# Order of the four array tiles in the seven-product steps, and moved query and key turns, in a thresholded-attention and bilinear-FFN kernel

## The chip, the cores and the metric

The kernel runs on one core of a Trainium2 chip. The metric is the device time of one execution in microseconds (us). The core has a matrix engine (PE, with its weight loads shown apart as PEld), a vector engine (DVE), an activation engine (ACT), a general engine (POOL) and a sync engine (SP) that here issues nearly all DMA transfers. Each engine works through its own instructions in program order, and waits for semaphores that others raise.

## The reference

Everything is 32-bit float. There are 8 batches, 8 heads, 576 positions and 64 columns a head.

```python
scores = scale * np.matmul(q, k.transpose(0, 1, 3, 2))
thresh = np.max(scores, axis=-1, keepdims=True) - tau
scores = np.where(scores >= thresh, scores, -1000000000.0)
attn = np.exp(scores - np.max(scores, axis=-1, keepdims=True))
attn = attn / (np.sum(attn, axis=-1, keepdims=True) + 1e-09)
x = np.matmul(attn, v)          # then (B,H,S,D) -> (4608, 512)
out = (x @ w_a) * (x @ w_b) @ w_out   # 512 -> 1536 -> 512
```

## The kernel before

**Units and slots.** Two heads of one batch make a pair, 32 pairs in all. A pair has 576 query rows: four blocks of 128, and a tail of 64 that it shares with its neighbour pair in one more block (block number `NT`). This gives 144 units (pair, block). The main loop runs over slots `g`; slot `g` computes the scores of unit `g` and works on older units: `turn_blocks` of unit `g-1`, `turn_back` of `g-2`, and the product with v (`weighted`) with a lag of three slots. The first eight units (`g < BY_PE`) turn their weights on PE (`turn_pe`), all later ones through DVE and a DMA to DRAM and back.

**A slot's attention work.** `scores` (matmuls at L404) writes two PSUM tiles. DVE takes the row maxima (L411), ACT the exponentials (L432), DVE applies the threshold mask and sums (L435, in `weigh`), DVE inverts the sums (L448), ACT scales (L454), DVE transposes in 32x32 blocks (L502), SP moves the result to DRAM (`swap`) and back (`wT`). `product` (L546) multiplies with v, and `settle` copies the result out of PSUM (ACT L553, DVE L554).

**Keys and queries.** For the first four pairs, `prep_pe` turns q and k on PE (L378) and `prep_copy` copies them from PSUM on DVE (L383). For all later pairs `prep` is one DVE transpose in place (L365) of a tile that SP loaded some slots earlier; q is turned one slot before its first use (the second half of an odd pair two slots before), k two slots before. In program order the q turn stands behind `turn_blocks` and ahead of the masks of the same slot, and the k turn stands behind the masks and ahead of the FFN work of that slot's second portion.

**FFN.** The FFN is a generator that `advance` moves on by a number of columns in several portions of each slot. A block is 256 rows of x. Plain products are at L828, with copy and multiply at L834 and L836. From the second group of batches on, two thirds of the first layer use the seven products of a 2x2 scheme (`sevens_of`, matmuls at L724, sums at L756 to L798, with L789, L794 and L798 on DVE). The second layer does so too (L894, sums at L857). At the end, when attention is done, only FFN remains.

**The array in four tiles.** Nearly all matmuls have 64 rows and 64 output columns, so they use one quarter of the 128x128 array: row half `r` (which partitions are read) and column half `c` (which output partitions are written). One step of `product` in `sevens_of` issues four matmuls, in the order (r,c) = 00, 01, 10, 11, with 128 columns each. Each 32-bit matmul of the program appears in the trace as two records.

**What sets the order.** The program order is fixed: `keep_order` ties each instruction to the one before it on its engine. PSUM has four tiles of two banks, handed out by `banks` in program order; a matmul into a reused tile waits for the engines that read it last. SP's transfers are queued by `post` and let out by `pump` as PE's columns pass.

**Tails of the first four pairs.** `parts(i, NT)` lists two products with v, one for each pair of a pair of pairs, with 32 moving columns in each matmul (`width` is 64 for the two row halves together).

Of the kernel before, what the change touches and what calls it, by code (L numbers as in the profile page):

```python
# [34 lines left out]
RAWS = 4  # L35
# [19 lines left out]
def kernel(  # L55
# [38 lines left out]
    nc = tc.nc  # L94
# [69 lines left out]
    def flush(*keys):  # L164

        while any(key in keys for key, _, _ in bulk):
            pump(1, False)
# [86 lines left out]
    def load_weights(limit, engine=nc.sync, most=NPIECES):  # L254

        behind = None
        if most < NPIECES:
            behind = next(x.name for x in reversed(nc.cur_bb.bb.instructions) if x.engine == mybir.EngineType.PE)
        while most and (len(raws) - len(taken) < limit or extra) and state["loaded"] < state["due"]:
            most -= 1  # L260
            n = state["loaded"]
            if len(raws) - len(taken) < limit:
                raw = work.tile([P, CW, 2], U32, tag="xT", bufs=XT_BUFS, name="raw")
            else:
                raw = taken[n] = extra.pop(0)
            src = pieces[n][1]
            for r, part in enumerate(src):
                dst = raw.rearrange("p f w -> p (f w)")[r * D:r * D + P // len(src)]
                if len(src) == 2:
                    dst = dst.rearrange("p (k f) -> p k f", k=2)  # L270
                moved = engine.dma_start(dst, part)
                if behind and r == 0:
                    tc.add_manual_dep(
                        moved.ins, behind,
                        mybir.DependencyInfo(mybir.DependencyClass.Sync, mybir.DependencyReason.DATA),
                        reason="pace")
            raws[n] = raw
            state["loaded"] = n + 1
# [103 lines left out]
    def prep_copy(mT, tp):  # L382
        nc.vector.tensor_copy(mT.rearrange("p (c k) -> p c k", c=2), tp)  # L383
# [56 lines left out]
    def reciprocal(i, u, engine):  # L440
        ws, sums = weights[i, u]
        n = len(ws)
        if engine is nc.scalar:
            nc.scalar.activation(sums[:, 0:n], sums[:, 0:n], AF.Copy, bias=1e-9)
        else:
            nc.vector.tensor_scalar_add(sums[:, 0:n], sums[:, 0:n], 1e-9)
        rcp = small.tile([P, 2], FP32, tag="rcp", name="rcp")
        nc.vector.reciprocal(rcp[:, 0:n], sums[:, 0:n])  # L448
        weights[i, u] = (ws, rcp)
# [38 lines left out]
    def parts(i, u):  # L488

        if i < HP:  # L490
            return {1: [(i, 0)], 3: [(i, 1)], NT: [(i, 2), (i + 1, 2)]}.get(u, [])
        return {1: [(i, 0)], NT if i % 2 == 0 else 3: [(i, 1)]}.get(u, [])

    def width(i, h):
        return (HALF, HALF, TAIL)[h] if i < HP else (HALF, HALF + TAIL)[h]

    def turn_blocks(i, u):

        ws, _ = weights.pop((i, u))
        t = whole.pop((i, u))  # L500
        for w in ws:
            nc.vector.transpose(w, w)  # L502
        swap = scratch.tile([G, P, NSLOT * Q], FP32, tag="swap" if u < NT else "swapt", name="swap")
        swaps[i, u] = swap
        for g in range(G):
            if u < NT:
                moves = [(swap[g].rearrange("(r p) e -> p r e", p=Q),
                          t[g * Q:(g + 1) * Q].rearrange("p (r s) e -> p r (s e)", r=G))]
            else:
                moves = []  # L510
                for m in range(2):
                    j = g // 2 ^ m
                    moves.append((swap[2 * m + g % 2, j * D:(j + 1) * D].rearrange("(r p) e -> p r e", p=Q),
                                  t[g * Q:(g + 1) * Q, m * NB:(m + 1) * NB].rearrange("p (r s) e -> p r (s e)", r=2)))
            post(("tw", i, u), *moves)
# [78 lines left out]
    def weighted_unit(i, u):  # L594
# [10 lines left out]
        if hp == HP - 1:  # L605
            state["rows"] = u + 1
            if u == 0:
                blocks.append(((x_of[b, 0], state["xs"]), ("first", b, 0)))

    def weighted(i, h):  # L610

        b, hp = pairs[i]
        flush(("v", i), ("wT", i if i >= HP or h < 2 else i - i % 2, h))
        n = width(i, h)
        if h < 2:
            groups = G + (n > HALF)
            wT = [turned.pop((i, 2 * h + y))[:, 0:groups] for y in range(2)]
        else:
            t = turned[i - i % 2, NT]
            wT = [t[:, i % 2 * 2 + y:i % 2 * 2 + y + 1] for y in range(2)]  # L620
            if i % 2:
                del turned[i - 1, NT]
        pv = product([lambda rows, s, t=t: t[rows, :, s] for t in wT], loaded[i]["v"], n)
        read = [], []
        settled_of[i] = settled_of.get(i, 0) + n
        if settled_of[i] == S:
            del loaded[i], prepared[i]
        if h < 2:
            if hp == 0:
                x_of[b, h] = x_tile("xT")  # L630
            settle(x_of[b, h][:, hp, :], pv, 0, P, read)
            settled[b, h] = hp + 1
            if hp == HP - 1:
                del settled[b, h]
                complete.append((x_of.pop((b, h)), ("half", b, h)))
        if n % HALF:
            t = b % GT
            if hp == 0 and t == 0:
                xtail_of[b // GT] = x_tile("xt")
            settle(xtail_of[b // GT][:, hp, t * TAIL:(t + 1) * TAIL], pv, (n - TAIL) // 2, n // 2, read)  # L640
            if hp == HP - 1 and t == GT - 1:
                complete.append((xtail_of.pop(b // GT), ("tail", b - t, 0)))
# [40 lines left out]
    def sevens_of(x, hg, plain):  # L683
# [29 lines left out]
        def product(m, out, fresh, last, groups=two):  # L713
            w, moving = products[m]
            nf = 2 * len(groups)
            left = whole = nf * HP * P
            for f in range(nf):
                g, y = groups[f // 2], f % 2
                for k in range(HP):
                    for r in range(2):  # L720
                        rows = slice(r * D, (r + 1) * D)
                        for c in range(2):
                            w0 = y * P + c * D
                            nc.tensor.matmul(out[c * D:(c + 1) * D, r, f * P:(f + 1) * P],  # L724
                                             w[g][k][rows, w0:w0 + D], moving[k][rows],
                                             start=(fresh and k == 0 and f == 0),
                                             stop=(k == HP - 1 and f == nf - 1),
                                             skip_group_check=True)
                    left -= P
                    if left:  # L730
                        yield P, left, whole
# [359 lines left out]
    for g in range(len(units) + PV_LAG):  # L1091
# [37 lines left out]
            advance(PORTIONS[0] * pace)  # L1129
        if g > BY_PE and g <= len(units):  # L1130
            turn_blocks(*units[g - 1])
        for p in range(HP, NPR):
            for name, d in (("q0", 1), ("q1", 1)):
                if g == (second if name == "q1" else first)[p] - d - (name == "q1" and p % 2):
                    prep(p, name)
        load_weights(RAWS if g < 9 else 3, most=1)
        if here:
            weigh(i, u)
        if here and g < BY_PE:
            reciprocal(i, u, nc.vector)  # L1140
        if 0 < g <= BY_PE:
            turn_pe(*units[g - 1])
        if g < 3:
            prep_copy(*prep_pe(g + 1, "k"))
        for p in range(HP, NPR):
            for name, d in (("k", 2),):
                if g == (second if False else first)[p] - d:
                    prep(p, name)
        if g > BY_PE:
            n = g - PV_LAG  # L1150
            held = 0.0
            now = parts(*units[n]) if BY_PE <= n < len(units) else []
            if now:
                held = 384 - (PORTIONS[2] + PORTIONS[3]) * pace + NSLOT * sum(width(*x) for x in now) // 2
                held = min(max(held, 0.0), 384)
            advance(PORTIONS[1] * pace - held)
            for p, h in now:
                if pairs[p][1] == 0:
                    make_x(2 if h == 1 and p >= HP and pairs[p][0] % GT == 0 else 1)
                make_room()  # L1160
                weighted(p, h)
                passed(NSLOT * width(p, h) // 2)
                running["owed"] -= NSLOT * width(p, h) // 2
            if back and back[0] > 0 and units[g - 2] != (0, NT):
                turn_back(*units[g - 2])
# [89 lines left out]
```

## Time and profile before

| what | value |
|---|---|
| median of 3 runs | 1408.98 us (1406.78 to 1411.38) |
| device time of the profiled execution | 1411.51 us |
| its span in the trace | 1409.7 us |
| PE busy, instructions | 1363.7 us (97%), 33980 matmul records |
| DVE busy | 1019.9 us (72%) |
| ACT busy | 678.2 us (48%) |
| POOL busy | 492.8 us (35%) |
| granted TensorE clock, mean | 0.999 |

Busy time is the union of an engine's instructions. Matmuls are pipelined and four run side by side, so the mean length of one (269 ns for 128 columns) is not what it costs; the distance between starts is. "Idle before" and "waits" name the engine or transfer whose semaphore came last. Times in the trace are counted from the start of the span.

### The profile page before, as it was taken

The page shows a single profiled execution, that of the slowest core. Times are in us where ns is not written, and L with a number is a line of the kernel's source. Part 1 is how long each engine was busy: PE and PEld are TensorE (multiplying, and loading weights), DVE is VectorE, ACT ScalarE, POOL GpSimd, SP SyncE. Part 2 cuts the span into 40 slices and gives each one's busy share as a digit, 9 for nine tenths or more (in the row PEclk, how much of TensorE's full clock was granted, in tenths as well). Part 3 has the DMA queues.
Part 4 walks back from the last instruction along what each step waited for, and adds up shares of the span by engine and source line. Part 5 has one row for each costly group of instructions (what it writes and reads, how often), then busy time and mean ns, then how long its engine had stood idle before and what let it go on. Part 6 is the DMA issues. An engine that isn't in the chain of part 4 may idle for free.

```text
span 1409.7 us, 76575 instructions
## 1 busy us (share of the span) xinstructions
PE 1363.7 (97%) x33980; PEld 1242.7 (88%) x33980; DVE 1019.9 (72%) x2212; ACT 678.2 (48%) x1245; POOL 492.8 (35%) x675
## 2 busy tenths in 40 slices
PE   6789999999999999999999999999999999999998
PEld 5678577899889899899997899998899899799998
DVE  6999877787777878776767776777777776745424
ACT  5887555545554555544444545454545455431110
POOL 2774442424150606060515142331515060708100
PEclk9999999999999999999999999999999999999999
DMA  9977776667666775675555765567655775550000
GB/s 206 241 209 221 202 211 160 177 167 191 175 155 162 195 196 150 172 199 152 142 149 145 191 168 154 137 165 184 181 137 148 201 191 152 136 153 18 4 19 18
DMA packets 327450, 223.23 MB, mean 158 GB/s; under 512 B 171600, under 2 KB 311632, under 8 KB 327120
## 3 DMA queue, kind: packets, MB, share of 16 engines
q1 hardware_dynamic: 323936, 216.95, 59.4%
q8 instruction: 268, 4.39, 1.3%
q10 hardware_dynamic: 3184, 1.38, 0.4%
q14 instruction: 62, 0.51, 0.1%
HBM read 128.58 MB, written 89.65 MB: 155 GB/s over the span
## 4 chain that ended last, share of the span: by engine, by line
PE 88%; DVE 5%; DMA 3%; SPq 2%; issue 1%; ACT 1%; DVEq 0%; ACTq 0%
PE pab L724 29%; PE po L894 21%; PE pab L828 18%; PE sc L404 10%; PE pv L546 9%; SPq L144 1%; DVE tw L435 1%; DVE mx L411 1%; DMA raw<-in_moe_w_b_dram 1%; DMA raw<-in_moe_w_a_dram 1%; DMA wT<-swap 1%; DVE low L311 1%; DVE tw L502 1%; DMA kT<-in_k_dram 0%; PE tp L483 0%
## 5 line engine op out<-in xcount | busy, mean ns | idle before, releaser
L454 ACT ACTIVATE tw<-tw,rcp 128x576 f32<-128x576 f32 x272 | 196.0, 768 | 211.8 <-DVE rcp L448 211.8
L411 DVE TENSOR_REDUCE mx<-sc 128x1 f32<-128x576 f32 x288 | 204.6, 751 | 119.3 <-PE sc L404 118.7
L432 ACT ACTIVATE tw<-sc,bias,scalars 128x576 f32<-128x576 f32 x288 | 239.4, 831 | 10.6 <-DMA qT<-in_q_dram 0.7
L686 POOL TENSOR_TENSOR h<-h,u 128x512 f32<-128x512 f32 x28 | 35.1, 1277 | 597.5 <-DVE h L798 416.0
L435 DVE SCALAR_TENSOR_TENSOR tw<-sc,thr,tw 128x576 f32<-128x576 f32 x288 | 220.3, 796 | 9.9 <-ACT tw L432 9.8
L894 PE MATMUL po<-wo_sb,h 64*64 64x256 f32 (+1 forms) x3408 | 212.9, 367 | 0.0
L502 DVE STREAM_TRANSPOSE tw<-tw 128x576 f32<-128x576 f32 x272 | 194.4, 752 | 0.8 <-ACT tw L454 0.8
L894 PEld LDWEIGHTS po<-wo_sb,h 64*64 64x64 f32 x3408 | 169.7, 133 | 16.6
L404 PE MATMUL sc<-kT,qT 64*64 64x288 f32 x2016 | 176.1, 404 | 4.3 <-DVE xt L554 1.4
L546 PE MATMUL pv<-wT,vm 64*64 64x128 f32 (+3 forms) x5040 | 167.4, 273 | 4.0 <-issue 3.4
L546 PEld LDWEIGHTS pv<-wT,vm 64*64 64x64 f32 x5040 | 156.5, 133 | 13.3 <-issue 7.9
L894 PE MATMUL po<-sums_u,h 64*64 64x256 f32 x2448 | 157.8, 376 | 0.8 <-DVE h L836 0.8
L857 POOL TENSOR_TENSOR h<-h 128x256 f32<-128x256 f32 x168 | 117.2, 731 | 111.7 <-PE po L894 100.4
L724 PE MATMUL pab<-xU,wb_sb 64*64 64x128 f32 x4352 | 139.4, 269 | 0.7 <-issue 0.7
L894 PEld LDWEIGHTS po<-sums_u,h 64*64 64x64 f32 x2448 | 125.4, 133 | 14.2 <-DVE h L836 1.3
L724 PEld LDWEIGHTS pab<-xU,wb_sb 64*64 64x64 f32 x4352 | 133.9, 133 | 3.3 <-issue 1.2
L404 PEld LDWEIGHTS sc<-kT,qT 64*64 64x64 f32 x2016 | 107.1, 133 | 26.2 <-issue 6.8
L431 ACT ACTIVATE bias<-mx,scalars 128x1 f32<-128x1 f32 x288 | 82.7, 287 | 63.3 <-DVE mx L411 62.8
L553 ACT COPY xT<-pv 128x128 f32<-128x128 f32 (+1 forms) x68 | 17.6, 258 | 198.2 <-PE pv L546 198.2
L724 PE MATMUL pab<-xS,wa_sb 64*64 64x128 f32 x2176 | 107.7, 269 | 0.0
L554 DVE COPY xT<-pv 64x128 f32<-64x128 f32 (+1 forms) x136 | 38.1, 280 | 82.2 <-PE pv L546 80.6
L535 ACT COPY kept<-po 128x512 f32<-128x512 f32 x65 | 34.8, 535 | 120.9 <-PE po L894 107.0
(159 smaller groups left out, 2470.4 us busy)
## 6 DMA issues: line engine op xcount, KB each, us to landing
wT<-swap SPq DMA_DIRECT2D x242, 288.0 KB, 3.8
swap<-tw SPq DMA_DIRECT2D x480, 144.0 KB, 3.1
vm<-in_v_dram SPq DMA_DIRECT2D x128, 72.0 KB, 2.2
swap<-tw SPq DMA_DIRECT2D x128, 72.0 KB, 3.0
kT<-in_k_dram SPq DMA_DIRECT2D x112, 72.0 KB, 3.3
wT<-swap SPq DMA_DIRECT2D x56, 144.0 KB, 3.4
out_dram<-kept SPq DMA_DIRECT2D x27, 256.0 KB, 3.6
qT<-in_q_dram SPq DMA_DIRECT2D x112, 40.0 KB, 2.5
```

Source lines behind the costliest of these rows:

```text
L404: nc.tensor.matmul(sc[m][o * D:o * D + wide, c], qT[r, q0:q0 + wide], kT[r, c * SH:(c + 1) * SH], start=True, stop=True)
L411: nc.vector.tensor_reduce(mx[:, c], sc[j], axis=AX.XY, op=ALU.max)
L431: nc.scalar.activation(bias[:, j:j + 1], mx[:, j:j + 1], AF.Copy, scale=e_nscale)
L432: nc.scalar.activation(wb[j], sb[j], AF.Exp, bias=bias[:, j:j + 1], scale=e_scale)
L435: nc.vector.scalar_tensor_tensor(out=wv, in0=sb[j], scalar=thr[:, j:j + 1], in1=wv, op0=ALU.is_ge, op1=ALU.mult, accum_out=sums[:, j:j + 1])
L454: nc.scalar.activation(w, w, AF.Copy, scale=rcp[:, j:j + 1])
L502: nc.vector.transpose(w, w)
L546: nc.tensor.matmul(pv[c * D:(c + 1) * D, y], vm[rows, s], wT[y](rows, s), start=(s == 0), stop=(s == NSLOT - 1))
L724: nc.tensor.matmul(out[c * D:(c + 1) * D, r, f * P:(f + 1) * P], w[g][k][rows, w0:w0 + D], moving[k][rows], start=(fresh and k == 0 and f ...
L828: nc.tensor.matmul(pab[c:c + columns(), r], w[rows, f // n, k, fs + c:fs + c + columns()], moving, start=(k == 0), stop=(k == H - 1))
L857: (nc.vector if state["over"] else nc.gpsimd).tensor_tensor(*a, **kw)
L894: nc.tensor.matmul(po[c * D:(c + 1) * D, r, y, cut], ht[rows, t0:t0 + D], other[rows, f, cut], start=(f == 0), stop=(f == NF // 2 - 1))
```

## The change

Four edits, in the order of the diff.

1. The tails of the first four pairs: two products of 36 matmuls with 32 moving columns become one of 36 matmuls with 64 (`weighted_tails`), in two places. The copies out of PSUM change from two on ACT (128x32) and four on DVE (64x32) to two and two of 64x64.
2. In a step of the seven products the four tiles come in the order 00, 11, 01, 10. The number of matmuls and their operands stay.
3. `prep` of q comes behind the weight load and the masks of its slot; `prep` of k comes behind the FFN work of the slot's second portion (and ahead of the product with v).
4. In slots 0 to 2, the PE turn of the next key stands ahead of `turn_pe`, and its copy out of PSUM is on ACT, where it was behind `turn_pe` and on DVE.

On PE, ACT, POOL and SP the instruction streams are otherwise in the same order as before; on DVE only the turns and copies named change place.

```diff
-            return {1: [(i, 0)], 3: [(i, 1)], NT: [(i, 2), (i + 1, 2)]}.get(u, [])
+            return {1: [(i, 0)], 3: [(i, 1)], NT: [(i, 2)]}.get(u, [])
...
-        return (HALF, HALF, TAIL)[h] if i < HP else (HALF, HALF + TAIL)[h]
+        return (HALF, HALF, 2 * TAIL)[h] if i < HP else (HALF, HALF + TAIL)[h]
...
+    def tails(x, pv, hp, c0, c1):
+        copies = [(nc.scalar.copy if j == c else nc.vector.tensor_copy)(
+            x[j * D:(j + 1) * D, hp + c, c0:c1], pv[c * D:(c + 1) * D, j]) for c in range(2) for j in range(2)]
...
+    def weighted_tails(i):
+        b, hp = pairs[i]
+        flush(("v", i), ("v", i + 1), ("wT", i, 2))
+        t = turned.pop((i, NT))
+        pv = banks(TAIL, "pv")
+        for s in range(NSLOT):
+            for j in range(2):
+                rows = slice(j * D, (j + 1) * D)
+                for c in range(2):
+                    nc.tensor.matmul(pv[c * D:(c + 1) * D, j], loaded[i + c]["v"][rows, s],
+                                     t[rows, 2 * c:2 * c + 2, s], start=(s == 0), stop=(s == NSLOT - 1))
...
                 for k in range(HP):
-                    for r in range(2):
+                    for r, c in ((0, 0), (1, 1), (0, 1), (1, 0)):
                         rows = slice(r * D, (r + 1) * D)
-                        for c in range(2):
-                            w0 = y * P + c * D
-                            nc.tensor.matmul(out[c * D:(c + 1) * D, r, f * P:(f + 1) * P],
...
+                        w0 = y * P + c * D
+                        nc.tensor.matmul(out[c * D:(c + 1) * D, r, f * P:(f + 1) * P],
...
+        load_weights(RAWS if g < 9 else 3, most=1)
+        if here:
+            weigh(i, u)
         for p in range(HP, NPR):
             for name, d in (("q0", 1), ("q1", 1)):
                 if g == (second if name == "q1" else first)[p] - d - (name == "q1" and p % 2):
                     prep(p, name)
-        load_weights(RAWS if g < 9 else 3, most=1)
-        if here:
-            weigh(i, u)
         if here and g < BY_PE:
             reciprocal(i, u, nc.vector)
+        if g < 3:
+            kT, tp = prep_pe(g + 1, "k")
+            nc.scalar.copy(kT.rearrange("p (c k) -> p c k", c=2), tp)
         if 0 < g <= BY_PE:
             turn_pe(*units[g - 1])
-        if g < 3:
-            prep_copy(*prep_pe(g + 1, "k"))
-        for p in range(HP, NPR):
-            for name, d in (("k", 2),):
-                if g == (second if False else first)[p] - d:
-                    prep(p, name)
...
             advance(PORTIONS[1] * pace - held)
+            for p in range(HP, NPR):
+                for name, d in (("k", 2),):
+                    if g == (second if False else first)[p] - d:
+                        prep(p, name)
             for p, h in now:
```

More of the change, by code (lines that the diff above doesn't have):

```diff
@@ L608, in weighted_unit @@
                 blocks.append(((x_of[b, 0], state["xs"]), ("first", b, 0)))
+    def tails(x, pv, hp, c0, c1):
+        copies = [(nc.scalar.copy if j == c else nc.vector.tensor_copy)(
+            x[j * D:(j + 1) * D, hp + c, c0:c1], pv[c * D:(c + 1) * D, j]) for c in range(2) for j in range(2)]
+        for n, a in enumerate(copies):
+            for m, b in enumerate(copies[:n]):
+                if (n in (0, 3)) != (m in (0, 3)):
+                    tc.declare_no_dep(a.ins, b.ins, reason="partitions of their own")
+    def weighted_tails(i):
[9 more added lines that the diff above has]
+                                     t[rows, 2 * c:2 * c + 2, s], start=(s == 0), stop=(s == NSLOT - 1))
+        if hp == 0 and b % GT == 0:
+            xtail_of[b // GT] = x_tile("xt")
+        t = b % GT
+        tails(xtail_of[b // GT], pv, hp, t * TAIL, (t + 1) * TAIL)
+        for p in (i, i + 1):
+            settled_of[p] = settled_of.get(p, 0) + TAIL
+            if settled_of[p] == S:
+                del loaded[p], prepared[p]
     def weighted(i, h):
+        if i < HP and h == 2:
+            return weighted_tails(i)
         b, hp = pairs[i]
-        flush(("v", i), ("wT", i if i >= HP or h < 2 else i - i % 2, h))
+        flush(("v", i), ("wT", i, h))
         n = width(i, h)
[L615 to L622, printed above, removed]
+        groups = G + (n > HALF)
+        wT = [turned.pop((i, 2 * h + y))[:, 0:groups] for y in range(2)]
         pv = product([lambda rows, s, t=t: t[rows, :, s] for t in wT], loaded[i]["v"], n)
@@ L719, in product @@
                 for k in range(HP):
-                    for r in range(2):
+                    for r, c in ((0, 0), (1, 1), (0, 1), (1, 0)):
                         rows = slice(r * D, (r + 1) * D)
-                        for c in range(2):
-                            w0 = y * P + c * D
[L724 to L728, printed above, removed]
+                        w0 = y * P + c * D
+                        nc.tensor.matmul(out[c * D:(c + 1) * D, r, f * P:(f + 1) * P],
+                                         w[g][k][rows, w0:w0 + D], moving[k][rows],
+                                         start=(fresh and k == 0 and f == 0),
+                                         stop=(k == HP - 1 and f == nf - 1),
+                                         skip_group_check=True)
                     left -= P
```

## The prediction

> **What bounds the kernel now.** I read the page first (engines, slices, chain), then the groups of PE by shape, PE's timeline in two places, the waits of DVE, and the timeline of single slots.
>
> ```profile
> span 1409.7 us, 76575 instructions
> ...
> PE 1363.7 (97%) x33980; PEld 1242.7 (88%) x33980; DVE 1019.9 (72%) x2212; ACT 678.2 (48%) x1245; POOL 492.8 (35%) x675
> ...
> DMA  9977776667666775675555765567655775550000
> ...
> PE 88%; DVE 5%; DMA 3%; SPq 2%; issue 1%; ACT 1%; DVEq 0%; ACTq 0%
> ```
>
> PE is the bound, and DMA is full in the first two slices (to 70 us). What a matmul costs is the distance between starts, read from the timeline of PE in the last stage (L724) and around three units' scores (L404):
>
> ```profile
> 1293.96 0.27 PE L724 MATMUL pab<-xT,wa_sb 64*64 64x128 f32 x1
> 1293.96 0.31 PE L724 MATMUL pab<-xS,wa_sb 64*64 64x128 f32 x3
> 1294.07 0.27 PE L724 MATMUL pab<-xT,wa_sb 64*64 64x128 f32 x1
> 1294.07 0.31 PE L724 MATMUL pab<-xS,wa_sb 64*64 64x128 f32 x3
> ...
> 225.85 1.15 PE L404 MATMUL sc<-kT,qT 64*64 64x288 f32 x16
> 233.30 1.15 PE L404 MATMUL sc<-kT,qT 64*64 64x288 f32 x16
> ```
>
> Four records, one on each tile of the array, start together, and the next four come 0.109 us later. Such a quartet takes 0.058 us at 64 columns, 0.109 at 128, 0.136 at 160, 0.216 at 256 and 0.2425 at 288 (starts in the trace). Counting all 33980 records at these rates gives 1322 us. The other 88 us of the span are stalls: 57 before 200 us, 31 after, and those 31 lie in some forty places of 0.1 to 1.6 us, not in the rate.
>
> Three kinds of stall concern the change. A late transfer holds DVE at a turn, and the FFN's copies behind it hold a PSUM tile that the next scores need:
>
> ```profile
> DVE qT L365 <- DMA qT<-in_q_dram: 7.0, 7, 1.8
> ...
> DVE kT L365 <- DMA kT<-in_k_dram: 4.9, 3, 2.1
> ```
> ```profile
> 959.54 0.78 DVE L365 STREAM_TRANSPOSE kT<-kT 128x576 f32<-128x576 f32 x1 [2.11 <-DMA kT<-in_k_dram]
> ...
> 960.24 1.18 DVE L789 TENSOR_TENSOR h<-h,pab 128x1024 f32<-128x1024 f32 x1
> ...
> 961.48 0.95 PE L404 MATMUL sc<-kT,qT 64*64 64x288 f32 x11 [1.15 <-DVE h L789]
> ```
>
> In the first slots scores wait for the key's copy, and the second tail product waits for a PSUM tile:
>
> ```profile
> 15.07 0.73 DVE L383 COPY kT<-tp 128x576 f32<-128x576 f32 x1
> ...
> 15.87 2.30 PE L404 MATMUL sc<-kT,first_u 64*128 64x288 f32 x8 [3.09 <-DVE kT L383]
> ```
> ```profile
> 121.12 1.25 PE L546 MATMUL pv<-sums_u,vm 64*64 64x32 f32 x72
> ...
> 123.50 1.35 PE L546 MATMUL pv<-sums_u,vm 64*64 64x32 f32 x72 [1.13 <-ACT h L834]
> ...
> 160.38 2.30 PE L546 MATMUL pv<-wT,vm 64*64 64x32 f32 x144
> ```
>
> **Part 1, the tile order: 0 us.** It touches all of L724: 15232 records in 3808 quartets, 3808 x 0.109 = 415 us. Each tile keeps its own work, so in a steady stretch only the phase between tiles can move. That the new order runs at full rate is shown once: a unit made of two pairs' tails issues its scores in exactly the order 00, 11, 01, 10. The unit at 233.30 is such a one, the one at 225.85 has 00, 10, 01, 11, and both take 1.15 us for 16 records. So zero is taken from the nearest row, though that row has 288 columns and L724 has 128, where weight loads come more than twice as often. Bounds: below, the part of a quartet that does not grow with columns (0.2158 - 2 x 0.1067 = 2.4 ns, from 256 against 128 columns), 3808 x 2.4 ns = 9 us of gain; above, one more start step (7 ns between neighbours in a quartet) each time, 3808 x 7 ns = 27 us of loss.
>
> [...]
>
> **Part 2, the turns of q and k: -2.2 us.** No instruction is added. 56 turns of q (0.40 to 0.51 us) go behind two masks (L435, 0.8 us each), 28 turns of k (0.77 us) behind the FFN's DVE work. SP's transfers keep their order, so no transfer starts elsewhere. Gains, by the stalls of PE in the trace: at 449.1, 933.5 and 1091.9 a q transfer held the masks for 1.2 to 1.8 us and the scores then waited for the masked tile (0.46, 0.33 and 0.73 us); at 818.2, 961.5 and 1119.2 a k transfer held L789 or L794 for 0.8 to 2.1 us (0.50, 1.35 and 1.0 us). Together 4.4 us; I take 3.4, since behind the FFN work the k turn still stands ahead of the copies of the product with v (L554), which the same scores wait for. Loss: the next scores need the q that now ends when the second mask ended before. In 50 of 56 slots that mask ended 0.3 us or more before the next scores, so nothing is late. In six it ended after they began (by 0.09 to 0.68 us). In three of those the masks now fill the time in which q is awaited; the others (154.0, 333, 482) cost 0.7, 0.2 and 0.3 us, 1.2 in all. Elsewhere the cover is the 0.3 to 3.5 us between mask and scores; if it went, 56 x 0.45 = 25 us would be at stake. What waits behind k on DVE is L554, then the inversions (L446, L448), for which ACT's L454 waits; its block is turned only in the next slot, where DVE waited for L454 once (0.8 us in all). Net -2.2, range -4.4 to +1.2.
>
> **Part 3, keys in slots 0 to 2: -0.8 us.** ACT's copy (0.64 us, as the first key's at L1069) follows the second exponential (ends 13.69), so scores start near 14.4 instead of 15.87: -1.5. In slot 2 the scores no longer wait for the copy at 24.2 but for the masks of slot 1 (22.94 less 1.5): about -3. Slot 3 likewise: -3.9. But these slots also convert weights that arrive at a fixed pace, one half piece each 1.1 us from 25 to 70 us, DMA full. In slot 4 ACT reads its third piece at 48.10, and that piece landed at 47.38. So ACT can be 0.7 us earlier there, and no more; its exponentials follow. I take 0.8; with all cover wrong it is 3.9, with transfers later still 0. ACT's three copies (1.9 us) stand ahead of the conversions that wait for the same pieces.
>
> **Part 4, tails: -1.9 us.** 288 records become 144. The first place loses a block of 1.35 us; its wait for L834 passes to the FFN's next matmul (L828), which takes that PSUM tile. Counted 1.3. The second falls from 2.30 to about 1.2 us (64 columns: 72 records in 1.28, at 39.73), but a DMA wait follows at 172.5 (1.1 us), behind SP, which issues without a break from 153 to 170; counted 0.6. Four DVE copies (0.8 us) become two. Range 0 to -2.4.
>
> **Sum.** 0 - 2.2 - 0.8 - 1.9 = -4.9 us, on the profiled span 1409.7 to 1404.8. That execution took 1411.51, 1.8 more than its span and 2.5 over the median; from the median 1408.98 the forecast is 1404.1 (-0.35%). A measurement of this kernel can tell about 0.3% (4.2 us) from no change; the runs shown spread over 0.33%.
>
> **Rivals.**
>
> *Hidden anyway, 1408 us.* Late transfers fall elsewhere in each execution, the first slots are held by the weights' arrival, and what is gained before 175 us is spent in SP's unbroken issues. Each term then goes to its small end. For it: the six stalls are 0.3% of the span, and instruction waits ("issue" in the waits of PE) move with any edit. Against: the order of DVE's work takes away the cause, not the instance. Chance 0.29.
>
> *The order costs, 1413 us and up.* At 128 columns the new order sets two tiles of one column half side by side (11 then 01, 10 then 00). If the second's load or start has to wait once in a quartet, each ns costs 3.8 us over 3808 quartets; from 2.4 ns the gain is eaten and the result is slower than before by over 0.3%; at 7 ns it is 1431. For it: no row shows this order at 128 columns. Against: scores in the order 00, 10, 01, 11 have the same neighbours and run at full rate, though at 288. Chance 0.13, with 0.03 for k turns that delay what follows.
>
> *The order gains, 1395 us.* [...] Chance 0.05.
>
> **How the numbers follow.** Forecast 0.50, order gains 0.05: faster by over 0.3% in 0.55. Hidden: same in 0.29. Slower 0.16. The range 1396 to 1413 reaches from the order's gain to the order costing 2.3 ns a quartet, and leaves out less than 2 in 10. The forecast's own range is 1400 to 1406.
>
> **What would show it.** L724 quartets still 0.109 us apart and its share of the chain still 29%; the waits of scores for L789 and L435 gone after 400 us; DVE's waits for qT and kT still there; L404 starting near 14.4 and 21.5 us and near 44 in slot 5 (44.77 before); one block of 72 records at 64 columns for each tail pair. Wrong it is if L724's quartets change length, if scores wait for qT (L365) in many slots, or if the time before 200 us grows.

## The result, and the profile after

| | median | runs | ratio to before, 95% interval |
|---|---|---|---|
| before | 1409.51 us | 20 (1403.16 to 1414.93) | |
| after | 1405.84 us | 20 (1399.65 to 1411.96) | 0.9969 [0.9955, 0.9984] |

By the ratio the change makes the kernel 4.4 us faster (2.3 to 6.3 by the interval; the two medians differ by 3.7); 4.9 us had been forecast. The profiled execution after took 1404.49 us (span 1402.7). Line numbers of PE's groups move: L724 becomes L749, L828 L853, L894 L919, L834 L859, and the new tails are L629.

From the page of the kernel after:

```profile
span 1402.7 us, 76307 instructions
...
PE 1366.8 (97%) x33836; PEld 1266.0 (90%) x33836; DVE 1012.2 (72%) x2205; ACT 680.6 (49%) x1248; POOL 492.5 (35%) x675
...
PE 91%; DVE 3%; DMA 3%; SPq 1%; issue 1%; ACT 1%; ACTq 0%; DVEq 0%
```

PE has 144 records fewer. Its idle time falls from 46.0 to 35.9 us (span less busy time) while its busy time grows by 3.1, and its share of the chain that ended last rises from 88 to 91%: in these two profiles the time went out of waits.

The timeline of PE in the last stage (start, length, count of records):

```profile
1293.00 0.27 PE L749 MATMUL pab<-xT,wa_sb 64*64 64x128 f32 x1
1293.06 0.28 PE L749 MATMUL pab<-xS,wa_sb 64*64 64x128 f32 x3
1293.11 0.56 PE L749 MATMUL pab<-xT,wa_sb 64*64 64x128 f32 x12
1293.44 0.27 PE L749 MATMUL pab<-xS,wa_sb 64*64 64x128 f32 x1
```

Twelve records from 1293.11 to 1293.44 are three quartets of 0.11 us. Over the whole trace, four records in a steady stretch take 109.35 ns in the old order and 109.34 in the new one (mean of 14131 and 14128 distances).

DVE's waits for the moved turns:

```profile
DVE kT L365 <- DMA kT<-in_k_dram: 1.2, 3, 0.5
...
DVE qT L365 <- DMA qT<-in_q_dram: 0.6, 1, 0.6
```

Before they were 4.9 and 7.0 us. They stay, as forecast, but are much shorter: the masks and the FFN work now stand ahead, and by the time the turn comes the transfer has mostly landed. No wait of the scores for L789's successor or for L365 is left in the list of PE's waits.

The first slots, PE and ACT:

```profile
13.96 2.30 PE L404 MATMUL sc<-kT,first_u 64*128 64x288 f32 x8 [1.49 <-ACT kT L1168]
...
18.77 4.11 PE L483 MATMUL tp<-first_u,tw 128*64 128x128 f32 x36 [0.41 <-DVE first_u L383]
22.81 1.41 PE L404 MATMUL sc<-kT,first_u 64*128 64x288 f32 x8
```
```profile
13.27 0.63 ACT L1168 COPY kT<-tp 128x576 f32<-128x576 f32 x1
```

The first tail place, PE:

```profile
119.44 1.28 PE L629 MATMUL pv<-sums_u,vm 64*64 64x64 f32 x72
121.81 1.13 PE L853 MATMUL pab<-xT,wb_sb 64*128 64x256 f32 x8 [1.09 <-ACT h L859]
```

One block where two stood, and the wait for ACT's L859 now falls on the FFN's next matmul, both as forecast.

### The profile page after: what moved, and what is told of

Read it like the earlier page. It is cut to its first block, busy times and chain, and to the rows that moved or that the text cites. A ratio compares the mean times of both kernels' runs of the same rounds, so it can differ in the third digit from the quotient of the medians.

```text
span 1402.7 us, 76307 instructions
## 1 busy us (share of the span) xinstructions
PE 1366.8 (97%) x33836; PEld 1266.0 (90%) x33836; DVE 1012.2 (72%) x2205; ACT 680.6 (49%) x1248; POOL 492.5 (35%) x675
## 4 chain that ended last, share of the span: by engine, by line
PE 91%; DVE 3%; DMA 3%; SPq 1%; issue 1%; ACT 1%; ACTq 0%; DVEq 0%
PE pab L749 30%; PE po L919 22%; PE pab L853 18%; PE sc L404 10%; PE pv L546 10%; SPq L144 1%; DMA wT<-swap 1%; DMA vm<-in_v_dram 1%; DVE mx L411 1%; DMA raw<-in_moe_w_b_dram 1%; PE tp L483 1%; DVE low L311 0%; DVE tw L435 0%; DVE tw L502 0%; DMA swap<-tw 0%
## 5 line engine op out<-in xcount | busy, mean ns | idle before, releaser
L919 PE MATMUL po<-wo_sb,h 64*64 64x256 f32 (+1 forms) x3408 | 210.7, 367 | 0.0
L919 PEld LDWEIGHTS po<-wo_sb,h 64*64 64x64 f32 x3408 | 172.3, 133 | 12.5
L404 PE MATMUL sc<-kT,qT 64*64 64x288 f32 x2016 | 170.6, 404 | 1.3 <-issue 0.9
L546 PE MATMUL pv<-wT,vm 64*64 64x128 f32 (+2 forms) x4896 | 165.0, 276 | 4.0 <-DMA wT<-swap 2.5
L919 PE MATMUL po<-sums_u,h 64*64 64x256 f32 x2448 | 156.7, 376 | 0.0
L919 PEld LDWEIGHTS po<-sums_u,h 64*64 64x64 f32 x2448 | 128.2, 133 | 10.2 <-DVE h L861 0.5
L749 PE MATMUL pab<-xU,wb_sb 64*64 64x128 f32 x4352 | 137.0, 269 | 0.0
L749 PEld LDWEIGHTS pab<-xU,wb_sb 64*64 64x64 f32 x4352 | 132.2, 133 | 2.5 <-ACT h L805 0.5
L749 PE MATMUL pab<-xS,wa_sb 64*64 64x128 f32 x2176 | 109.1, 269 | 0.0
```

The source lines that it names most:

```text
L404: nc.tensor.matmul(sc[m][o * D:o * D + wide, c], qT[r, q0:q0 + wide], kT[r, c * SH:(c + 1) * SH], start=True, stop=True)
L546: nc.tensor.matmul(pv[c * D:(c + 1) * D, y], vm[rows, s], wT[y](rows, s), start=(s == 0), stop=(s == NSLOT - 1))
L919: nc.tensor.matmul(po[c * D:(c + 1) * D, r, y, cut], ht[rows, t0:t0 + D], other[rows, f, cut], start=(f == 0), stop=(f == NF // 2 - 1))
```

## The experiments

All ratios are to the kernel before, run beside them on the same chip. "Singles" have one edit of the four.

**The order alone.**

```diff
-                    for r in range(2):
+                    for r, c in ((0, 0), (1, 1), (0, 1), (1, 0)):
```

> Only the tile order of the seven products is changed (part 1). Theory (the order is free, the gain comes from DVE's turns, the keys and the tails): the L724 quartets stay 0.109 us apart and the time is that of the kernel before within 2 us. Rival 'the order gains': the 2.4 ns that do not grow with columns go, up to 9 us faster. Rival 'the order costs': slower by 3.8 us for each ns that a quartet grows, seen as a longer distance between quartets. A third possibility after the trace of the changed kernel, where the last stage lost about 2 us in stalls of 0.25 us: 1 to 3 us slower, with the distance inside steady stretches unchanged.

Measured 1412.21 us against 1410.00, ratio 1.0011 [0.9997, 1.0025]. Four records take 109.37 ns. No gain, and any cost lies below 3.5 us.

**The turns alone** (edit 3 of the diff).

> Only the turns of q and k after the first four pairs are moved on DVE (part 2). Theory: 2.2 us faster (0 to 4.4), DVE's waits for kT and qT (7.0 and 4.9 us before) shrink to under 3 us together, and the scores' waits for L789, L435 and late L554 go. Rival 'hidden anyway': within 1 us of the kernel before, the stalls of scores only change place. Rival 'q too late': scores wait for L365, slower by up to 1.2 us or more.

Measured 1409.32 against 1410.00, ratio 0.9982 [0.9960, 1.0004]: 2.5 us less by the ratio, with no gain at all just inside the interval. DVE's waits for kT and qT are 3.1 and 0.9 us, 4.0 together and not under 3. After 400 us one long wait of the scores for the FFN's sums is left: 1.23 us at 494.6 for DVE's L777, which stands behind a k turn (L365) whose transfer held it for 1.84 us. So the new place of the k turn can still hold the FFN.

**The keys alone** (edit 4).

> Only the keys of slots 0 to 2 are turned ahead and copied on ACT (part 3). Theory: the scores of slots 1, 2 and 3 start 1.5 to 4 us earlier, but from slot 5 on 0.8 us is left, since the weights' pieces land at a fixed pace; total 0.8 us faster. Rival 'transfers do not bind': 3 to 4 us remain at slot 10 and in the total. Rival 'nothing': no lead is left by slot 6, and the total is unchanged.

Measured 1409.46 against 1410.00, ratio 0.9996 [0.9976, 1.0017]. The scores of slot 1 start at 13.95 instead of 15.87, those of slot 5 at 43.39 instead of 44.77, those of slot 6 at 54.57 instead of 54.67: gained and given back. What took it back in this execution is not shown to be the weights' transfers: from 44.4 to 51.2 us, between the starts of slots 5 and 6, PE has half its clock (see part 3 below).

**The tails alone** (edit 1).

> Only the tails of the first four pairs are made one product of 64 columns (part 4). Theory: 1.9 us faster (0 to 2.4): about 1.3 us lead after the first place (slot 14) and 2 us after the second (slot 20), kept to the end. Rival 'SP binds there': the lead is gone at slot 22, since SP issues without a break from 153 to 170 us; total unchanged.

Measured 1404.98 against 1410.00, ratio 0.9969 [0.9956, 0.9982]: 4.4 us less, the size of the whole change. Only 1.9 had been counted, so the next runs look at this term.

**Everything but the order.**

> The changed kernel with the old tile order 00, 01, 10, 11 in the seven products; tails, turns and keys stay changed. Theory (the order is free): the same time as the changed kernel within 2 us, about 1405.5, quartets at 128 columns 0.109 us apart. Rival (the order costs a little, as the run with the order alone hints, 1412.2 against 1410.0): 1.5 to 3 us below the changed kernel run beside it, about 1403.

Measured 1403.98 against 1408.97, ratio 0.9970 [0.9957, 0.9983].

**The changed kernel again**, beside it.

> The changed kernel once more, beside the others on the same chip. Both theories: about 4.4 us below the kernel before (ratio 0.9969, between 0.9955 and 0.9984).

Measured 1405.51, ratio 0.9977 [0.9959, 0.9996]. By these two ratios the order costs 1.0 us, by the single above 1.5. Both lie inside their errors: no gain, and a cost of 1 to 2 us can't be excluded.

**Each tail product twice.**

```diff
-        for s in range(NSLOT):
+        for s in list(range(NSLOT)) * (2 if n == TAIL else 1):
```

> The kernel before, with each tail product of the first four pairs issued twice into the same PSUM tile: 288 more records of 32 columns, 1.25 + 1.35 + 2.30 = 4.9 us of PE work in the two places. Theory (time of PE at these places counts once, with its own length): 4.9 us slower than before, 4 to 6. Rival (a shift at these places is worth more than its length, because transfers after it then hold or do not hold the scores; the tails alone gained 4.4 us where 1.9 was counted, a factor of 2.3): 11 us slower. Second rival (PE waits there for transfers anyway): 0 to 2 us slower.

Measured 1426.11 against 1408.97, ratio 1.0121 [1.0099, 1.0144]: 17 us more, beyond even the rival. The timeline of PE at the first place shows why:

```profile
122.74 3.73 PE L546 MATMUL pv<-sums_u,vm 64*64 64x32 f32 x220
128.25 1.93 PE L546 MATMUL pv<-sums_u,vm 64*64 64x32 f32 x68 [1.78 <-issue]
130.10 2.08 PE L828 MATMUL pab<-xT,wb_sb 64*128 64x256 f32 x8
```

After 220 short records in a row PE stands still without a wait that the profile shows ("issue"), and the FFN block behind it takes 2.08 us where the trace of before has 1.13. The windows of the same kernel show the clock there (columns: length of the window, PE busy with its records, granted clock, DMA share, GB/s):

```profile
124.00:128.00 4.00, 2.40 (x148) 1.00 0.52 167
128.00:132.00 4.00, 3.75 (x78) 0.57 0.96 267
132.00:136.00 4.00, 4.00 (x23) 0.58 0.39 135
136.00:140.00 4.00, 4.00 (x40) 1.00 0.25 58
```

The granted clock is at half speed for 6.8 us here, and for 3.4 us again at 176.3, behind "issue" stalls of 1.40 and 2.19 us in the second place. The stretch from the scores of slot 13 to those of slot 14 grows from 8.39 to 13.00 us, the one from slot 18 to 20 from 15.81 to 22.52. So the doubling does not measure what one tail block is worth: most of it is a stall and a clock loss that the kernel before does not have at these places in its profile. It does show 288 more short records costing 17 us where their length was counted as 4.9.

**Four steps of a tile in a row.**

```diff
-                for k in range(HP):
+                for k0 in range(0, HP, 4):
...
+                            for k in range(k0, k0 + 4):
```

> The kernel before, with four steps of a tile in a row in the seven products: sixteen matmuls in the order 00 four times, 01 four times, 10 four times, 11 four times, where four tiles took turns. Theory (each tile has a queue of its own that can run several steps ahead, so the order within a step can't matter): the same within 4 us, 1408 to 1414. Rival (PE starts matmuls strictly in program order, so four steps of one tile stand one behind the other): the 952 groups of 16 matmuls go from 4 x 0.22 us towards 16 x 0.22, so between 1500 and 3500 us.

Measured 1919.50, ratio 1.3632 [1.3589, 1.3676]. The theory fell: no steady four at 109 ns is left. The timeline of PE in this kernel:

```profile
1000.23 0.27 PE L725 MATMUL pab<-xS,wa_sb 64*64 64x128 f32 x1
1000.28 0.27 PE L725 MATMUL pab<-xT,wa_sb 64*64 64x128 f32 x1
1000.34 0.27 PE L725 MATMUL pab<-xS,wa_sb 64*64 64x128 f32 x1
1000.39 0.27 PE L725 MATMUL pab<-xT,wa_sb 64*64 64x128 f32 x1
```

One record starts every 0.055 us and two streams alternate, where before four records started together each 0.109: two tiles at work, not four. So the order of matmuls does decide the rate in this kernel: 1919.50 us against 1411.26 with two steps in a row (below).

**The tails and the turns alone**, a candidate for a better version.

> The changed kernel without the tile order and without the keys' move: tails and turns alone. Theory (tails carry the gain, turns add 1 to 2 us, keys and order nothing): 1403 to 1404.5, ratio near 0.9965, the same as the changed kernel or up to 2 us below. Rival (the edits gain only together, by all shifting the same late transfers): no better than the tails alone run beside it, near 1405, and the changed kernel's keys would be what is missing.

Measured 1404.51 against 1410.08, ratio 0.9963 [0.9948, 0.9978]. The same as the changed kernel within the error; keys and order are not needed for the gain, and no version beats the changed kernel by more than could be measured.

**The tails alone, again.**

> The tails alone once more (it measured 4.4 us below the kernel before, between 2.5 and 6.2, where 1.9 had been counted). Theory A (the tails free only PE's time at the two places, 1.2 and 1.3 us as its trace showed): 2 to 3 us below before. Theory B (more comes with it: a half-clock window of 3.4 us that two of four profiles with the old tails have at the first place and none of four with the new ones): 4 to 5 us below before.

Measured 1406.55 against 1410.08, ratio 0.9971 [0.9948, 0.9994], 4.1 us less: the median repeats, though the interval holds both theories.

**Thinner tails.** Four of nine position groups are left out of each tail product of the first four pairs.

```diff
-        for s in range(NSLOT):
+        for s in range(0, NSLOT, 2 if n == TAIL else 1):
```

> The kernel before, with five of the nine position groups in each tail product of the first four pairs and the other four left out of the sum: 160 records of 32 columns instead of 288, copies and order unchanged. Theory (what counts is the number of short records on PE at these two places): 128 x 17.4 ns = 2.2 us less by the rate alone, and up to 4 to 5 us less if stalls and half-clock windows go with them as with the tails alone. Rival (the gain of the tails came from the copies, 4 on DVE and 2 on ACT against 2 and 2, or from the place of the copy in the queues): 0 to 1 us less.

Measured 1409.90 against 1410.08, ratio 1.0009 [0.9991, 1.0027]. The theory fell: 128 short records fewer bring nothing that can be measured. PE's timeline at the first place:

```profile
119.33 0.79 PE L546 MATMUL pv<-sums_u,vm 64*64 64x32 f32 x40
121.70 0.94 PE L546 MATMUL pv<-sums_u,vm 64*64 64x32 f32 x40 [1.58 <-ACT h L834]
122.57 2.08 PE L828 MATMUL pab<-xT,wb_sb 64*128 64x256 f32 x8
```

The first block is 0.46 us shorter than before (0.79 against 1.25), and the wait for L834 behind it 0.45 longer (1.58 against 1.13): that gain is waited away. The second block gains 0.41, and in this execution half the clock is gone from 122.4 on (2.08 for the FFN block), which hides that gain. So fewer short records ahead of the wait for L834 bring nothing; that the gain of the fused tails comes from having nothing of them behind that wait fits these lines, but was not tested alone. The rival, that the copies carry part of the gain, is open too: they were not varied alone.

**Two steps of a tile in a row.**

> The kernel before, with two steps of a tile in a row in the seven products (four in a row gave 1919.5, 0.134 us more for each quartet of 128 columns). Theory (PE starts ahead of program order by a few matmuls only, so overlap is lost from the point where one tile has more in a row than that): two steps lie between, 1430 to 1750. Rival (looking ahead reaches over two steps of 8 matmuls): 1405 to 1415.

Measured 1411.26 against 1410.08, ratio 1.0006 [0.9981, 1.0030]; four records in a steady stretch take 109.5 ns. The rival holds: with two steps (16 records in a cycle over the tiles) PE still fills all four tiles, and with four steps it does not.

## Why the prediction was right, point by point

The forecast of 4.9 us stands well inside the measured 2.3 to 6.3. That it came within half a microsecond is partly luck: by the singles the terms are +1.5 (order), -2.5 (turns), -0.6 (keys) and -4.4 (tails), -6.0 in all, each with an interval of 2 to 3 us to either side, where 0, -2.2, -0.8 and -1.9 were counted.

The signs promised were seen, with one exception: in slot 2 the scores start at 22.81, not near 21.5, since PE itself was still busy with a turn of weights (L483, 18.77 to 22.88). With the changed kernel run again they start at 20.77, and there the same 36 records of L483 take 2.19 us instead of 4.11: early in the kernel PE works at half its pace (8 records of scores take 2.30 us in slot 1 and 1.25 in slot 2 of the kernel before), and the moment when the pace doubles differs from execution to execution. In slot 5 it was 42.84 and 44.85 in these two, so the sign "near 44" was too fine to read from one profile.

The two profiles of the tails alone differ by 6.2 us in their span, so the terms are read from stretches between the scores of two slots, over all thirteen profiles of kernels at the normal rate (each edit is in some of them). The differences are means with against means without the edit, with their standard error; where a doubled or thinned tail would disturb a stretch, that kernel is left out.

| stretch | edit | without | with | difference |
|---|---|---|---|---|
| slot 13 to 14 | tails | 8.93 | 7.12 | -1.8 +- 0.3 |
| slot 18 to 20 | tails | 15.36 | 14.45 | -0.9 +- 0.4 |
| slot 0 to 13 | keys | 108.98 | 108.30 | -0.7 +- 0.6 |
| slot 14 to 18 | turns | 28.19 | 29.32 | +1.1 +- 0.1 |
| slot 20 to 24 | turns | 31.61 | 33.08 | +1.5 +- 0.7 |
| slot 24 to 64 | turns | 332.86 | 332.89 | 0.0 +- 0.6 |
| slot 64 to 139 | turns | 672.23 | 666.96 | -5.3 +- 1.1 |

One row mixes two edits. From slot 18 to 20, four of the six kernels with the new tails have the moved turns too. Taken apart, the means are 15.56 us with neither edit (4 profiles), 15.26 with the tails alone (2), 14.55 with the turns alone (1) and 14.05 with both (4). So the tails bring 0.3 to 0.5 us there and the turns 1.0 to 1.2; most of that row's -0.9 belongs to the turns.

**Part 1, the order, 0 us: right in the rate, with a reason that is too strong.** The steady rate is the same to 0.03 ns between the kernels, 0.1 us over 3808 quartets, so both bounds (9 us of gain, 27 of loss) were far too wide, and the rivals "the order costs" and "the order gains" fell as far as the rate goes. The reason given, that each tile keeps its own work, does not hold in general: four steps in a row cost 510 us. What the runs show is where the overlap ends: one cycle over the four tiles has 8 records and 8 loads in the usual order and 16 and 16 with two steps, and four records take 109.35 and 109.5 ns there; with four steps it has 32 and 32, and a single record starts only every 0.055 us. Why it breaks between 16 and 32 was not shown.

**Part 2, the turns, -2.2 us: the net was right within the error, both of its sides were too small.** The gain, taken as 3.4 of 4.4, is 5.3 +- 1.1 in the stretch where late transfers fall, and single places were only instances, as the rival "hidden anyway" had it: the six stalls moved from profile to profile, but with the old place DVE's wait for q is 3.2 to 10.0 us in all eight profiles, and 0.4 to 1.1 in all five with the new place. The first loss (0.7 at 154.0) came in full: the stretch from slot 17 to 18, whose scores start there, went from 7.49 to 8.33 us. In the changed kernel, DVE and PE:

```profile
150.85 0.82 DVE L435 SCALAR_TENSOR_TENSOR tw<-sc,thr,tw 128x576 f32<-128x576 f32 x1
...
151.59 0.44 DVE L365 STREAM_TRANSPOSE qT<-qT 128x256 f32<-128x256 f32 x1
```
```profile
152.13 1.32 PE L404 MATMUL sc<-kT,qT 64*64 64x288 f32 x16 [0.89 <-issue]
```

The q turn ends at 152.03 and the scores start 0.10 later. The wait is put down to "issue", but what ended last is the turn, which a list of waits alone would have hidden. By the means above, most of this loss comes back from slot 18 to 20. The two losses at 333 and 482 (0.5 us together) did not show, with an error of 0.6. What was not foreseen are 1.5 us between slots 20 and 24, where PE waits for the weights' way back from DRAM; in the changed kernel:

```profile
187.70 2.08 PE L546 MATMUL pv<-wT,vm 64*64 64x128 f32 x67 [1.34 <-DMA wT<-swap]
```

The transfers before it leave SP one behind the other (four loads of k from 178.71 to 182.82, then wT). This is the mechanism of the rival "hidden anyway": what PE gains before 175 us it partly spends here. Kernels with the old turns had such a wait too (slots 20 to 24 took 34.23 and 32.79 us with two steps and with thin tails), so it belongs to PE's lead over SP as much as to the turns; no run separates the two. The net of the four rows of the turns is -2.7, and near -3.8 with what comes back from slot 18 to 20; the single gave -2.5, with an error that covers both.

**Part 3, keys, -0.8 us: the number agrees, the reason did not hold.** The start of slot 1, counted from that of slot 0, moved by 1.6 (1.5 was worked out), and -0.7 +- 0.6 is left at slot 13, which is hardly clear of nothing. The cap was read from one landing time: the third piece of weights landed at 47.38 and ACT read it at 48.10, so ACT could be only 0.7 us earlier. But with the keys moved the piece itself was issued and landed earlier, at 45.26 in the changed kernel and 45.95 with the keys alone, and ACT read it at 46.12 and 46.67. So the pieces do not arrive at a pace of their own. What took the lead back in both of these profiles is 6.8 us of half clock (from 43.7 and 44.4): the stretch from slot 5 to 6 takes 11.18 us in them, and 9.90 both before and with everything but the order, where no such window falls there. In the changed kernel run again there was a wait of 2.89 us before 27.25 and half clock from 27.7, and no lead was left in slot 5. That the sum came out near 0.8 is luck.

**Part 4, tails, -1.9 us: the two places were nearly right, the time gained was more.** The first place gives 1.8 us (1.3 was counted), the second 0.3 to 0.5 with the turns held apart (0.6 was counted). The second block is a microsecond shorter, but, as part 4 said of SP, it is then the transfer that is waited for; with the tails alone:

```profile
162.03 1.21 PE L629 MATMUL pv<-wT,vm 64*64 64x64 f32 x67 [1.13 <-DMA wT<-swap]
```

At the first place three of five profiles with the old tails have 8.35 to 8.42 us there, 1.3 over the new ones, exactly the counted block, and two have 9.7 and 9.8, each with 3.4 us of half clock (from 122.9 and 125.5). That makes the other 0.5 of the mean. None of six profiles with the new tails has that there; with so few profiles, that the fused tails prevent it is likely and not shown. This is how such a window looks in the kernel with the order alone, to be held against 1.35 and 1.13 us of the same blocks before:

```profile
124.95 1.88 PE L546 MATMUL pv<-sums_u,vm 64*64 64x32 f32 x72 [1.11 <-ACT h L833]
126.77 2.08 PE L827 MATMUL pab<-xT,wb_sb 64*128 64x256 f32 x8
```

Before, the second of them:

```profile
124.78 1.13 PE L828 MATMUL pab<-xT,wb_sb 64*128 64x256 f32 x8
```

The profile before showed a clock of 1.00 at this place, so one execution could not tell of it. In time the tails alone gave 4.4 and 4.1 us (2.5 to 6.2 and 0.8 to 7.3 by the intervals), more than the 2.1 to 2.3 that the places show. The remaining 2 us were found in no stretch; whether they exist, and whether the changed copies have a part in them, stays open. By the medians of the single runs the tails are the largest term, the turns the second, where the forecast had them the other way round; the intervals of the two overlap.

## What to carry to other kernels

Fusing two small products into one wider one removes a whole block where a wait stands between them (1.3 us at the first place); ask what the second one waits for, since a mere shortening ahead of such a wait gave nothing here (ratio 1.0009 with the thinner tails). A turn that waits for a transfer belongs behind the work that others wait for, but work out its loss at the places where its own result is already late, and look there in the timeline rather than in the list of waits. A cap that is read from the landing time of a transfer moves when the kernel issues that transfer earlier (the third piece landed at 47.38 before and at 45.26 after); ask what its issue waits for. Terms of one to three microseconds are read from stretches between fixed points of several profiles, not from the difference of two spans, and with the other edits held apart.

## What the runs showed of the hardware that was not expected

**The granted clock was at half in windows of 3.4 or 6.8 us, some of them right behind a short stall.** Outside the last microseconds, the profile before has no such window, the one after two (6.8 us from 43.7 and 3.4 us from 77.8), the doubled tails five. In such a window an FFN block took 2.08 us where 1.13 is usual; by that, as an estimate, a window costs up to half its length where PE is busy. Two examples: they came behind a stall of 2.42 us in the kernel with the turns alone (its product at 190.12 took 3.69 us where 2.08 is usual), and of 3.41 us in the second run of the tails; in windows of the latter:

```profile
1100.00:1112.00 12.00, 12.00 (x356) 1.00 0.80 210
1112.00:1124.00 12.00, 8.59 (x163) 0.72 0.66 179
```

So a late transfer can cost more than its wait: in the first example 1.6 us on top of the 2.42. At the first tail place 1.1 us of idle time between short matmuls was followed by a window in some executions and not in others, and a stall of 3.14 us before 193.12 in the kernel with two steps was followed by none, so the length of the stall alone does not decide. What does decide it was not shown.

**Two steps of a tile in a row keep four tiles at work, four steps do not.** Two steps of a tile in a row (109.5 ns for four records) cost nothing, four in a row add 510 us to the 415 that these products had taken, with two tiles at work instead of four. Three were not tried, and no run shows what in PE sets the limit.

**Runs of short matmuls stalled in the kernel with the doubled tails.** 144 records of 32 columns in a row ran through in 2.30 us before; in the doubled tails 220 in a row were followed by a stall of 1.78 us put down to "issue", and at the second place 143 and 127 by stalls of 1.40 and 2.19. The traces point to the arrival of PE's instructions. In the profile, a DMA queue of kind "instruction" (q8) moves 268 packets of 16 KB in the kernel before and 270 with the doubled tails. The three stalls at the tails ended 1.27, 1.32 and 1.37 us after such a packet had landed (at 126.98, 169.52 and 173.83). Over the thirteen profiles, 35 of the 50 stalls of PE above 0.6 us that are put down to "issue" ended 1.2 to 1.65 us after one; a random moment does so in 9% of cases. So most of these stalls look like waits for instructions; no run varied that.
